# Reordering the first five steps of a fused attention and gated-convolution kernel: input transposes ahead of the attention output, output transposes one step later, weight preparation later

## Chip, cores and metric

One core of one Trainium2 chip. The metric is the device time of one execution in microseconds (us), the median of several executions. Engines: PE is TensorE (matrix products and transposes), PEld its weight loads, DVE is VectorE, ACT is ScalarE, POOL is GpSimd. DMA moves data between device memory and on-chip memory.

Runs carry a state. A run is called slow when it lies over 1.5% above the fastest run of the same kernel. Ratios below use fast runs alone, and compare with the kernel before in the same round; the rounds ran on different chips.

## The reference, cut to what matters

```python
def _attn_ref(q, k, v):                 # 8 batches, 8 heads, 576 positions, 64 wide
    scores = scale * np.matmul(q, k.transpose(0, 1, 3, 2))
    mask = block_i >= block_j           # causal in blocks of 64 positions
    scores = np.where(mask, scores, -1000000000.0)
    ...                                 # softmax over the last axis
    return np.matmul(attn, v)

def _moe_ref(x, w_val, conv_w, w_out):  # x: 8 x 576 x 512, from the heads side by side
    ...                                 # gate = sigmoid(causal convolution of 5 taps over positions)
    val = x @ w_val
    return (gate * val @ w_out)
```

The inputs and the result are float32.

## The kernel before

All instructions are issued in an order that the program fixes. One step `p` of 32 handles a pair of heads: three score tiles S0, S1 and S2 with their exponentials, the transposes of the next pair, and the attention output ("av") of the pair before. Half a batch of the convolution and the products with `w_val` and `w_out` follow from step 5 (`LAG`) on.

```python
def trans(p, bank): ...      # PE: 8 transposes of cast q and k; VectorE copies them into qkT
def s_tile(p, t): ...        # PE: score tile t; ScalarE: exponential into pt
def mask(p): ...             # GpSimd: two memsets on pt, after the third exponential of p
def av(p, banks): ...        # PE: 30 matmuls; VectorE: reciprocal and scaling, twice, into x16
def xtrans(p, bank): ...     # PE: 5 transposes of x16; VectorE copies them into xt
def trans_tails(b, bank):... # PE: 4 transposes of the last 64 positions of a batch; VectorE copies to kt
def s_last(b): ...           # last scores of a batch, and their exponential
def conv_weights(): ...      # PE turns the convolution weights, VectorE builds DG from them

def casts(p):                # all on GpSimd, in this order
    for i in (p + 1, p + 2):
        if ... and (p >= 5 or i == p + 1):
            cast_qk(i)       # q and k of a pair, 128x1024, float32 to float16
    cast_v(p)
    ...
    if p == 3 or (p > 0 and p % 4 == 0 and p + 4 < NP):
        cast_tails((p + 4) // 4, nc.gpsimd)
    if p in (6, 7):
        cast_w_out(p - 6)

for p in range(NP):          # NP = 32
    gs = p - LAG
    ...
    casts(p); s_tile(p, 0); s_tile(p, 1)
    ...                      # p == 0: warm-ups and tails instead of av
    av(p - 1, ...)
    trans(p + 1, 2)          # for 0 < p < 31
    ...                      # permute_w_out at 8, 9, 10; output tiles from 11 on
    s_tile(p, 2); mask(p)
    ...                      # p == 0: warm-ups, conv_weights, trans(1), last scores
    ...                      # even gs: convolution
    xtrans(p - 1, ...)
    if p in (5, 6):
        scale_w_val(2 * p - 10); scale_w_val(2 * p - 9)   # VectorE: w_val * 0.5 into w_val_sb
    ...                      # val, permute_w_out(1) at 8, tails, last scores at 4
```

`warm(n)` are n dummy matmuls that keep PE busy.

The softmax here doesn't subtract the row's maximum and nothing guards it: scores larger than these inputs give would overflow.

## Time and profile before

| | before |
|---|---|
| median of 3 runs | 198.56 us (198.2 to 198.68) |
| profiled run | 198.43 us, span 196.6 us, mean granted clock 0.996 |
| first score matmul of step 1, 5, 9, 31 | 14.26, 29.53, 52.10, 165.40 us |

How to read it: the span is cut into 40 equal slices of 4.9 us, one digit each, in tenths (9 means 90% or more). The row of the granted TensorE clock, from the page of the kernel before, is what the prediction did not show:

```profile
PEclk9999999999999999999999999999999999999998
```

The granted clock is 0.9 or more in every slice but the last, which has 0.8. The loop that the prediction finds in steps 2 to 4 shows on GpSimd. In the timeline of the kernel before the columns are start, duration, engine, line, operation, output and input, shape; the bracket is the idle time before and what ended it. L204 is the mask and L129 the cast of q and k.

```profile
21.70 0.41 POOL L204 MEMSET pt<- 64x384 f16 x1 [1.63 <-ACT pt L188]
22.32 1.04 POOL L129 CAST qk<-qks 128x1024 f16<-128x1024 f32 x1
...
25.62 0.41 POOL L204 MEMSET pt<- 64x384 f16 x1 [1.14 <-ACT pt L188]
```

From mask to mask 3.92 us pass.

### The profile page before, as it was taken

To read this page: it belongs to the slowest core of one execution; us is meant where nothing else is said; L and a number is where in the kernel's file an instruction comes from. 1 tells how busy PE (TensorE), PEld (TensorE's weight loads), DVE (VectorE), ACT (ScalarE), POOL (GpSimd) and SP (SyncE) were. 2 spreads that over 40 slices of the span, in tenths; PEclk is the share of its full clock that TensorE was granted. 3 is DMA by queue.
4 is the path that set the end of the run, shared out by engine and by line. 5 is a ranking of instruction groups with operands and counts; after the bars stand their busy time and mean duration, and the time that the engine had idled before them with its cause. 6 is when DMAs were issued, how large, how long until landed. Compare 5 with 4: busy or idle time off the path is not lost.

```text
span 196.6 us, 8730 instructions
## 1 busy us (share of the span) xinstructions
PE 183.3 (93%) x3714; PEld 124.4 (63%) x3714; DVE 130.8 (67%) x286; ACT 138.6 (71%) x192; POOL 83.5 (42%) x168
## 2 busy tenths in 40 slices
PE   2999878779899999999999999999999999999992
PEld 1456656557577676667766677677767676755550
DVE  4346785897678686777686877768676868642451
ACT  4438778758699778877888878887988787635321
POOL 7363664596444554345434644464445422100000
PEclk9999999999999999999999999999999999999998
DMA  5999999999899568876887687977775111124445
GB/s 155 256 286 265 250 274 323 312 215 278 242 224 253 171 174 217 255 228 186 236 232 234 189 240 212 276 216 207 220 213 146 57 56 58 58 107 165 163 160 213
DMA packets 70337, 40.43 MB, mean 206 GB/s; under 512 B 48149, under 2 KB 64789, under 8 KB 70298
## 3 DMA queue, kind: packets, MB, share of 16 engines
q1 hardware_dynamic: 69872, 39.46, 73.8%
q8 instruction: 29, 0.48, 1.0%
q10 hardware_dynamic: 426, 0.40, 0.6%
q14 instruction: 10, 0.08, 0.2%
HBM read 30.42 MB, written 9.44 MB: 203 GB/s over the span
## 4 chain that ended last, share of the span: by engine, by line
PE 80%; DVE 10%; POOL 3%; ACT 2%; DMA 2%; issue 1%; POOLq 0%; SPq 0%; DVEq 0%; ACTq 0%
PE G L33 51%; PE S L33 18%; PE G L154 6%; PE G L244 5%; DVE qkT L165 3%; DVE x L235 3%; DMA vs<-in_v_dram 2%; POOL qk L129 1%; ACT pt L188 1%; PE G L141 1%; DVE w_val L379 1%; DVE rc L234 1%; DVE gv L282 1%; POOL v L134 1%; POOL pt L204 1%
## 5 line engine op out<-in xcount | busy, mean ns | idle before, releaser
L188 ACT ACTIVATE pt<-S 128x1024 f16<-128x1024 f32 x96 | 95.0, 1024 | 21.4 <-PE S L33 19.1
L204 POOL MEMSET pt<- 64x384 f16 x32 | 13.5, 423 | 74.0 <-ACT pt L188 73.9
L33 PE MATMUL G<-xt,w_val 128*128 128x288 f16 x256 | 37.9, 286 | 0.3 <-DVE qkT L165 0.2
L165 DVE COPY qkT<-G 128x1024 f16<-128x1024 f16 x31 | 37.7, 1215 | 0.2 <-PE G L154 0.2
L129 POOL CAST qk<-qks 128x1024 f16<-128x1024 f32 x31 | 32.9, 1061 | 10.9 <-DMA qks<-in_k_dram 7.7
L33 PEld LDWEIGHTS <-pt 128*128 128x128 f16 x960 | 31.2, 97 | 8.6 <-issue 4.0
L33 PE MATMUL G<-w_out,gv 128*128 128x512 f16 x144 | 36.5, 379 | 0.0
L33 PE MATMUL G<-v,pt 128*128 128x65 f16 x896 | 34.1, 194 | 1.7 <-DVE gv L282 1.3
L282 DVE SCALAR_TENSOR_TENSOR gv<-th,G 128x288 f16<-128x288 f32 x64 | 28.2, 453 | 10.7 <-PE G L33 9.0
L304 ACT COPY osb<-G 128x512 f32<-128x512 f32 x31 | 18.2, 586 | 23.8 <-PE G L33 22.0
L235 DVE TENSOR_TENSOR x<-G,rc 128x320 f16<-128x320 f32 x64 | 31.5, 492 | 2.2
L33 PEld LDWEIGHTS <-qkT 64*128 64x128 f16 x496 | 16.0, 94 | 22.9 <-issue 16.8
L33 PE MATMUL S<-qkT 64*128 64x512 f16 (+1 forms) x248 | 28.5, 301 | 2.1 <-DVE qkT L165 1.1
L33 PEld LDWEIGHTS <-w_val 128*128 128x128 f16 x256 | 24.2, 98 | 8.5 <-issue 0.9
L234 DVE RECIPROCAL rc<-G 128x5 f32<-128x5 f32 x64 | 12.2, 190 | 22.6 <-PE G L33 22.5
L246 DVE COPY xt<-G 128x576 f16<-128x576 f16 x32 | 14.6, 455 | 13.5 <-PE G L244 13.2
L154 PE MATMUL G<-ident,qk 128*128 128x128 f16 x256 | 20.1, 222 | 0.2 <-POOL qk L129 0.2
L134 POOL CAST v<-vs 128x512 f16<-128x512 f32 x32 | 19.9, 621 | 0.5 <-DMA vs<-in_v_dram 0.3
L33 PEld LDWEIGHTS <-gv 128*128 128x128 f16 x144 | 12.9, 98 | 9.9
L33 PE MATMUL G<-xt,DG 32*32 32x288 f16 x640 | 17.2, 288 | 0.0
L33 PE MATMUL S<-xt,DG 32*32 32x288 f16 x640 | 17.1, 287 | 0.0
L154 PEld LDWEIGHTS <-qk 128*128 128x128 f16 x256 | 15.4, 100 | 1.3 <-POOL qk L129 0.4
(58 smaller groups left out, 151.8 us busy)
## 6 DMA issues: line engine op xcount, KB each, us to landing
out_dram<-osb SPq DMA_DIRECT2D x35, 256.0 KB, 2.1
qks<-in_q_dram SPq DMA_DIRECT2D x32, 256.0 KB, 4.2
vs<-in_v_dram SPq DMA_DIRECT2D x64, 128.0 KB, 4.4
qks<-in_k_dram SPq DMA_DIRECT2D x31, 256.0 KB, 4.3
tlst<-in_q_dram SPq DMA_DIRECT2D x8, 128.0 KB, 4.8
tlst<-in_k_dram SPq DMA_DIRECT2D x8, 128.0 KB, 4.6
vtst<-in_v_dram SPq DMA_DIRECT2D x8, 128.0 KB, 4.8
w_st<-in_moe_w_val_dram SPq DMA_DIRECT2D x2, 512.0 KB, 6.3
```

The costliest lines, as they stand in the source:

```text
L33: nc.tensor.matmul(out=out, lhsT=lhsT, rhs=rhs, start=start, stop=stop, skip_group_check=True)
L129: nc.gpsimd.tensor_copy(out=o, in_=s)
L134: nc.gpsimd.tensor_copy(out=v16s[p % NV][0:128, 0:4, 0:2, 0:64], in_=s)
L154: nc.tensor.transpose(out=r[:, o:o + 128], in_=t[0:128, c, 2 * i:2 * i + 2, 0:64], identity=ident16[0:128, 0:128])
L165: nc.vector.tensor_copy(out=o[0:128].rearrange("p i (s n) -> p i s n", n=4), in_=src)
L188: nc.scalar.activation(out=pts[p % NPT][0:128, 0:2, 512 * t:512 * t + 512], in_=s[0:128, 0:2, 0:512], func=AF.Exp, bias=0.0, scale=0.125)
L204: nc.gpsimd.memset(pt[64:128, 0:2, 0:1536].rearrange("p h (t s) -> p h t s", t=3)[:, :, :, 0:64], 0.0)
L234: nc.vector.reciprocal(out=rc[0:128], in_=O[:, :, 64:65])
L235: nc.vector.tensor_tensor(out=x[0:128, 0:5, h, 0:64], in0=O[:, :, 0:64], in1=rc[0:128].to_broadcast([128, 5, 64]), op=ALU.mult)
L246: nc.vector.tensor_copy(out=xts[b % NX][0:128, g, 4:4 + SEQ], in_=r[:, 0:SEQ])
L282: nc.vector.scalar_tensor_tensor(out=gv[u][0:128, x, bi, hf, 0:288], in0=t[0:128, x, 0:288], scalar=1.0, in1=r[0:128, 0:288], op0=ALU.add, ...
L304: nc.scalar.copy(out=o[0:128], in_=r[0:128, 0:512])
```

## The change

The intent: transposes of the next pair are issued ahead of av, so that VectorE copies them without first normalising av; output transposes are taken from the pair before last, so that PE doesn't wait for that normalisation. Convolution weights leave step 0, and the `w_out` work is moved later. The core of the diff, with cuts marked:

```diff
     def casts(p):
+        if p == 3 or (p > 0 and p % 4 == 0 and p + 4 < NP):
+            cast_tails((p + 4) // 4, nc.gpsimd)
         for i in (p + 1, p + 2):
 ...
-        if p == 3 or (p > 0 and p % 4 == 0 and p + 4 < NP):
-            cast_tails((p + 4) // 4, nc.gpsimd)
-        if p in (6, 7):
-            cast_w_out(p - 6)
 ...
+    for p in range(LAG):
+        loads(p)
+        casts(p)
+        s_tile(p, 0)
+        s_tile(p, 1)
+        if p == 0:
+            warm(2)
+            trans_tails(0, 0)
+        if p > 2:
+            trans_tails(p - 2, 0)
+        if p > 0:
+            trans(p + 1, 2)
+        if p > 1:
+            xtrans(p - 2, 3)
+        if p > 0:
+            av(p - 1, (0, 1))
+        s_tile(p, 2)
+        mask(p)
+        if p == 0:
+            trans(1, 2)
+            warm(2)
+        if p in (0, 3):
+            s_last(p // 3)
+        if p < 2:
+            warm(4 - 2 * p, 3)
+        if p == 2:
+            conv_weights()
 ...  # second loop, from step 5: as before, but
+        if 9 <= p <= 12:
+            permute_w_out(p - 9, 3)
+        if p > 12:
+            out(3)
 ...
+        if p in (7, 8):
+            cast_w_out(p - 7)       # after the mask
 ...
+        if p == 5:
+            scale_w_val(0)
+            scale_w_val(1)
 ...  # ahead of val in step 5; the other two after val in step 6
+        if p == 6:
+            scale_w_val(2)
+            scale_w_val(3)
```

## The prediction

> **What bounds the kernel now.** I read the page first: busy shares, then the forty slices.
>
> ```profile
> PE 183.3 (93%) x3714; PEld 124.4 (63%) x3714; DVE 130.8 (67%) x286; ACT 138.6 (71%) x192; POOL 83.5 (42%) x168
> ...
> PE   2999878779899999999999999999999999999992
> ...
> DMA  5999999999899568876887687977775111124445
> ```
>
> Over the whole span TensorE (PE) is the busiest engine, and from slice 13 on (about 59 us) its row is all nines. Before that it has 7s and 8s: these first nine or so steps ("step" p handles one pair of heads, 32 in all) are another regime, and the change touches only it. What the change is worth is therefore how much earlier or later the saturated stretch starts, plus or minus TensorE work moved across that border. DMA is also at nine tenths there, so input may arrive too late for a faster start.
>
> Next the busy time in stretches cut at the first score matmul of steps 1 to 9 (columns: PE, PEld, DVE, ACT, POOL, clock, DMA share, GB/s).
>
> ```profile
> 14.26:18.00 3.74, 3.51 (x63) 2.34 (x63) 2.47 (x6) 2.96 (x3) 0.15 (x1) 1.00 1.24 264
> 18.00:21.74 3.74, 2.97 (x59) 2.17 (x60) 2.77 (x7) 2.96 (x3) 2.04 (x5) 1.00 1.24 259
> 21.74:25.48 3.74, 3.24 (x63) 2.40 (x63) 2.77 (x7) 2.94 (x3) 2.67 (x5) 1.00 1.16 235
> 25.48:29.53 4.05, 3.49 (x72) 2.58 (x73) 3.35 (x9) 2.98 (x4) 3.33 (x6) 1.00 1.09 292
> ...
> 39.86:46.32 6.46, 5.05 (x149) 3.72 (x149) 5.47 (x11) 4.22 (x6) 5.07 (x9) 1.00 0.96 231
> ```
>
> No engine is full in steps 1 to 4, though each takes 3.74 to 4.05 us: a chain of waits sets the pace. PE idles 42.94 - 36.96 = 6.0 us between 14.26 and 57.20, the most that perfect ordering could win there. The chain of waits inside steps 2 to 4 names the loop:
>
> ```profile
> 22.32 1.05 POOL qk L129
> 23.37 0.05 issue
> 23.42 0.62 PE G L154 x8
> 24.04 0.35 PE S L33 x10
> ...
> 24.48 1.03 ACT pt L188
> ...
> 25.62 0.05 POOL pt L204
> ...
> 26.23 1.04 POOL qk L129
> ```
>
> GpSimd casts q and k of the next pair (L129), PE transposes them (L154), PE makes the third score tile S2, ScalarE takes its exponential, GpSimd masks it (L204, L206), and only then comes the next cast, because on GpSimd the mask of step p stands ahead of the cast of step p+1. From cast to cast: 26.23 - 22.32 = 3.91 us. (In steps 1 and 2 the VectorE loop of normalising and copying qkT costs nearly the same, 3.74.)
>
> [...] the transposes of step 3 start at 23.42 just after the cast ended at 23.37, and all later matmuls of the step come after them. [...] a transposition placed ahead of other matmuls makes these wait for its cast too. [...] the trace shows a cold start (four warm-up matmuls 1.89 us) and three later ones in 0.82; [...] so I expect no cold clock from fewer warm-ups. [...] one cast took 1.69 us instead of 1.04 while the convolution weights were built on VectorE (11.97 to 12.80).
>
> **The change, part by part.** The order of instructions in the built kernel confirms what the diff says: in steps 1 to 4 PE runs S0, S1, transposes of pair p+1, output transposes of pair p-2, attention output (av) of pair p-1, S2. GpSimd still has the mask of p-1 ahead of the cast of p+1.
>
> 1. Step 0. Convolution weights (about 1.0 us on PE) and 10 of 26 warm-up matmuls (0.22 to 0.27 us each, from 1.25 us for five and 0.82 for three) go. S0 of step 1 then starts when the filler has run: S2 of step 0 done 9.75, transposes 10.2, two warm-ups 10.65, last scores 10.9, four warm-ups 11.8. Before: 14.26. A head start of about **2.4 us**.
>
> 2. Steps 1 to 4. The good: qkT no longer waits for normalisation on VectorE (4 instructions, 0.20 + 0.49 + 0.18 + 0.49 us). The bad: in the loop above, between transposes and S2, there now stand five output transposes (0.3 us of issue) and av (30 matmuls, 1.0 us, 22.28 to 23.3). New loop: mask 0.65 with its wait, cast 1.05, wait 0.1, transposes 0.5, output transposes 0.3, av 1.0, S2 with its wait 0.5, exponential 1.02 = **5.1 us** against 3.9. In steps 3 and 4 the cast of the tails (0.62) is moved ahead of the cast, on the loop: 5.7. Ends of the third exponential, from 11.07 in step 0 (before: 11.26): step 1 15.9 (before 17.73), step 2 21.05 (21.58), step 3 26.7 (25.50), step 4 32.9 (29.41). The tails of step 4 land at about 28, which adds 0.4. The before side still spent 0.6 us on the last scores of batch 1 in step 4; I have these inside step 3. So after step 4 the changed kernel is some **2.7 us behind** at the first exponential of step 5 (32.9 against 30.23).
>
> 3. Steps 5 to 7. Most of that is given back, as the old kernel stalls here: GpSimd waits 2.37 us for qk of pair 7 (lands 33.5) and 2.08 for pair 8 (38.2), and step 7's av starts only at 41.77, after GpSimd had cast w_out (1.24) ahead of the mask and VectorE had scaled w_val (1.85) ahead of gv. The DMA stream is full and no load waits for a buffer, so landings stay. Behind by 2.7 us, the new kernel finds pair 7 nearly there. My walk: third exponential of step 5 ends 36.65 (before 33.70), of step 6 41.25 (39.0); mask of step 6 done 41.95, av at 42.3 against 41.77: **0.5 us behind**. Then the two moved w_val scalings (1.3 to 1.85) delay normalisation of step 7 and its convolution, which reuses the banks of av: **+0.9**.
>
> 4. Steps 8 to 12. Step 8 loses two w_out permutations (2 x 0.33) and the stall on their copy (0.69): 5.78 becomes about 4.4. First score matmul of step 9: 52.1 to 52.3, against 52.10. But the two permutations remain to be done in the saturated part: 0.66.
>
> 5. The end. Outputs start two steps later, so two more tiles (4 matmuls, 0.97 us each) sit in the tail. PE is full there too, so they only move: 0.
>
> Sum: 0.0 to 0.2 + 0.66 = about **+0.7 us**, 198.56 + 0.7 = 199.3.
>
> **Rivals.** (a) *The head start survives.* If transposes ran without waiting for the cast, steps 1 to 4 would go at the ScalarE pace (three exponentials, 3.0 us, plus gaps) and the 2.4 us of step 0 would be kept, perhaps with more of the 6.0 us of idle: 194 to 196.5. For it: qk of pairs 3 and 4 land at 14.2 and 16.9, long before use. Against: the fixed order on GpSimd. And pairs 7 and 8 land at 33.5 and 38.2 regardless; with casts blocking in order on GpSimd, nearly all of a lead would be waited away, so about 197. (b) *The delay persists.* If the deferred weights collide with steps 5 to 8 more than I see, 2.7 us of lag plus 0.9 stays: 201.5 to 202. For it: VectorE is at 5.47 of 6.46 us in step 7. Against: cast w_out no longer precedes the mask. (c) *Nothing moves:* DMA sets the start of saturation and both orders fit under it: 198.0 to 199.0. This is near to my own result.
>
> **Range and chances.** 2% is 4.0 us. Faster by that needs more than the whole step-0 gain and no DMA wait: 3%. Slower by it needs the entire lag to persist and grow: 5%. The range takes my walk's likely error of 2 us either way, a little more above since such a walk omits small waits: 197.0 to 202.0.
>
> **What would show it.** Step 1's S0 near 11.8; casts of q and k from step 2 on 5 us apart instead of 3.9, PE idle before the transposes of steps 2 to 4 released by the cast, 1 us or more each; third exponential of step 4 ending near 32.9; the GpSimd waits for pairs 7 and 8 shrinking from 2.4 and 2.1 to below 1; av of step 7 starting without a wait for gv; no wait on the copy of w_out near 51; all nines from about 52 us. Wrong would be: step intervals below 4 us in steps 2 to 4 (rival a), or step 9's scores after 54 us (rival b).

## The result

| | before | after |
|---|---|---|
| median of 4 runs each | 198.38 us | 204.10 us (203.28 to 205.35) |
| profiled run | 198.43 us, clock 0.996 | 205.35 us, clock 0.972 |
| first score matmul of step 1, 5, 9, 31 | 14.26, 29.53, 52.10, 165.40 | 12.08, 35.56, 57.52, 170.58 |

The ratio is 1.030, interval 1.024 to 1.037: slower. (A ratio is the mean time of one kernel's fast runs over that of the other's of the same rounds, so not quite the ratio of the medians.) All four runs of the changed kernel count as fast, with mean clocks of 0.972, 0.975, 0.958 and 0.983.

The page of the changed kernel: busy tenths of PE and the granted clock.

```profile
PE   3896677778999999999999999999999999999992
PEclk9997876999999999999999999999999999999999
```

The sevens of PE go further right than before, and the clock row has gained 7, 8, 7, 6 in slices 4 to 7. Next, stretches of the changed kernel, cut at the first score matmul of steps 1 to 4. The columns are stretch and length, then the busy time of PE, PEld, DVE, ACT and POOL with instruction counts, the clock, the DMA share and GB/s.

```profile
12.08:15.35 3.27, 2.95 (x59) 2.02 (x58) 1.65 (x3) 2.37 (x3) 1.49 (x2) 1.00 1.17 290
15.35:22.32 6.97, 5.33 (x68) 4.50 (x68) 3.59 (x9) 3.44 (x4) 2.16 (x4) 0.76 1.14 244
22.32:29.83 7.51, 4.79 (x72) 3.98 (x72) 4.27 (x9) 3.01 (x4) 3.09 (x5) 0.77 1.02 257
29.83:35.56 5.73, 4.57 (x63) 3.72 (x64) 2.71 (x6) 2.38 (x3) 3.27 (x6) 0.70 1.12 334
```

Where the kernel before took 3.74 to 4.05 us a step, steps 2 and 3 take 7.0 and 7.5. No engine is full in them, and the clock is at about three quarters on average. The chain of waits in step 3 (start, duration, what):

```profile
23.88 1.05 POOL qk L129
24.93 0.05 issue
24.98 0.99 PE G L154 x8
25.97 0.53 PE G L244 x5
26.50 1.65 PE G L33 x30
28.15 0.52 PE S L33 x10
...
28.75 1.03 ACT pt L188
```

This is the predicted loop with output transposes (L244) and av (30 matmuls, L33) between the transposes (L154) and S2. But the prediction had 0.5, 0.3 and 1.0 us for these three, and they took 0.99, 0.53 and 1.65. The granted clock in this trace has two values, 1.00 and 0.50, and changes between 18.24 and 35.30 us in pieces of 3.41 us. Cutting the changed kernel at their edges:

```profile
14.82:18.24 3.42, 1.78 (x21) 0.79 (x18) 1.25 (x5) 2.85 (x3) 2.12 (x4) 1.00 1.24 264
18.24:21.65 3.41, 3.41 (x51) 3.17 (x48) 2.83 (x6) 0.46 (x1) 0.04 (x1) 0.50 1.06 239
21.65:25.06 3.41, 1.76 (x19) 1.17 (x19) 1.43 (x3) 2.50 (x3) 2.66 (x5) 1.00 0.90 236
25.06:28.48 3.42, 3.42 (x53) 3.27 (x55) 2.41 (x6) 0.00 (x0) 0.42 (x1) 0.50 1.07 252
28.48:31.89 3.41, 1.47 (x27) 0.63 (x21) 0.70 (x2) 3.08 (x4) 1.93 (x4) 1.00 1.10 329
31.89:35.30 3.41, 3.13 (x43) 3.06 (x43) 2.18 (x5) 0.37 (x1) 1.34 (x3) 0.50 1.13 322
```

In these six windows the pattern alternates. In one PE waits for GpSimd and ScalarE and is busy for 43 to 52%. In the next it has the burst of transposes, output transposes, av and S2 to do, and does it at a clock of 0.50. The longest single PE idle in these steps is 1.39 us. In the kernel before the emptiest such window held 2.06 of 3.41 us (60%), and the clock was 1.00 in it and in the one after it:

```profile
38.22:41.63 3.41, 2.06 (x19) 1.11 (x19) 3.41 (x5) 2.55 (x4) 3.27 (x4) 1.00 0.95 257
```

How far each kernel is behind the kernel before (the start of a step's first score minus that of the kernel before; the last column is the difference of spans; one profiled run each). The profile of fill, in italics, is of a slow run: only its first two columns, ahead of its first half-clock window, are used.

| kernel | step 1 | step 5 | step 9 | step 31 | end |
|---|---|---|---|---|---|
| after | -2.2 | 6.0 | 5.4 | 5.2 | 6.9 |
| *fill* | -1.6 | 2.7 | 4.0 | 3.3 | 5.0 |
| av_first | -2.3 | 3.3 | 2.9 | 3.5 | 5.2 |
| before_swap | 0.6 | 4.1 | 4.0 | 3.9 | 3.9 |
| two_ahead | -1.6 | 3.7 | 3.2 | 4.2 | 6.0 |
| tails_last | -1.6 | 5.2 | 3.4 | 2.5 | 4.2 |
| undo_both | -2.3 | 0.8 | -1.6 | -2.0 | -0.2 |
| defer_only | 0.4 | 0.4 | -1.5 | -2.2 | -0.4 |
| delay | 0.0 | 2.8 | 0.3 | 0.2 | 0.2 |
| loop_fill | 0.1 | 3.5 | 3.3 | 4.6 | 4.7 |
| best1 | -2.3 | 0.2 | 1.0 | 1.4 | 3.1 |
| best2 | -1.8 | -1.6 | -2.6 | -2.4 | -0.7 |

### The profile page after: what moved, and what is told of

Same layout as the page of the kernel before. It is cut to its first block, busy times and chain, and to the rows that moved or that the text cites. A ratio compares the mean times of both kernels' runs of the same rounds, so it can differ in the third digit from the quotient of the medians.

```text
span 203.5 us, 8700 instructions
## 1 busy us (share of the span) xinstructions
PE 185.4 (91%) x3704; PEld 127.9 (63%) x3704; DVE 131.5 (65%) x286; ACT 138.4 (68%) x192; POOL 82.9 (41%) x168
## 4 chain that ended last, share of the span: by engine, by line
PE 77%; DVE 8%; DMA 5%; POOL 3%; ACT 3%; issue 2%; SPq 1%; POOLq 0%; DVEq 0%; ACTq 0%
PE G L33 47%; PE S L33 17%; PE G L154 6%; PE G L244 5%; DMA qks<-in_k_dram 5%; DVE qkT L165 3%; POOL qk L129 3%; DVE x L235 2%; ACT pt L188 2%; DVE gv L282 1%; DVE rc L234 1%; DVE w_val L377 1%; PE G L141 1%; POOL pt L206 0%; SPq L86 0%
## 5 line engine op out<-in xcount | busy, mean ns | idle before, releaser
L33 PE MATMUL G<-xt,w_val 128*128 128x288 f16 x256 | 38.2, 286 | 0.5 <-DVE qkT L165 0.4
L33 PEld LDWEIGHTS <-pt 128*128 128x128 f16 x960 | 33.7, 101 | 6.7 <-issue 4.5
L33 PE MATMUL G<-v,pt 128*128 128x65 f16 x896 | 36.3, 199 | 0.1
L33 PE MATMUL G<-w_out,gv 128*128 128x512 f16 x144 | 36.3, 379 | 0.0
L129 POOL CAST qk<-qks 128x1024 f16<-128x1024 f32 x31 | 32.3, 1043 | 4.9 <-DMA qks<-in_k_dram 3.4
L33 PE MATMUL S<-qkT 64*128 64x512 f16 (+1 forms) x248 | 29.0, 303 | 2.9 <-ACT pt L188 2.3
L33 PEld LDWEIGHTS <-qkT 64*128 64x128 f16 x496 | 16.1, 95 | 23.5 <-issue 18.9
L33 PEld LDWEIGHTS <-w_val 128*128 128x128 f16 x256 | 24.2, 98 | 8.9 <-issue 1.2
L154 PE MATMUL G<-ident,qk 128*128 128x128 f16 x256 | 20.9, 228 | 3.0 <-POOL qk L129 2.9
L33 PEld LDWEIGHTS <-gv 128*128 128x128 f16 x144 | 13.0, 98 | 10.1
L154 PEld LDWEIGHTS <-qk 128*128 128x128 f16 x256 | 15.9, 102 | 4.6 <-POOL qk L129 4.0
L33 PE MATMUL G<-xt,DG 32*32 32x288 f16 x640 | 17.2, 288 | 0.7 <-DVE x L235 0.3
L33 PE MATMUL S<-xt,DG 32*32 32x288 f16 x640 | 16.8, 287 | 0.1
```

The source lines that it names most:

```text
L33: nc.tensor.matmul(out=out, lhsT=lhsT, rhs=rhs, start=start, stop=stop, skip_group_check=True)
L129: nc.gpsimd.tensor_copy(out=o, in_=s)
L154: nc.tensor.transpose(out=r[:, o:o + 128], in_=t[0:128, c, 2 * i:2 * i + 2, 0:64], identity=ident16[0:128, 0:128])
```

## The experiments

Four questions: is the half clock a cause; which of the two reorderings (PE order, tails first) lengthens the loop; what happens to a lag in steps 5 to 8; and is there a version that beats both. Each edit is against the changed kernel unless it says otherwise.

### fill: dummy matmuls in the idle time of PE

```diff
         s_tile(p, 0)
+        if p == 4:
+            warm(4, 2)
         s_tile(p, 1)
 ...
+        if p > 1:
+            warm({2: 5, 3: 4, 4: 2}[p], 2)
         if p > 2:
             trans_tails(p - 2, 0)
+            warm(2, 2)
```

> The changed kernel with 15 dummy matmuls put where TensorE waits in steps 2 to 4 (5 ahead of the transposes of step 2; 4 and 2 around the tail transposes of step 3; 4 between the score tiles, 2 and 2 around the tail transposes of step 4). Nothing else moves. Theory A (the waits of the longer loop leave TensorE half idle for one clock window after another[...]): granted clock back to 0.99, no half-clock windows, third exponential of step 4 ending near 33 instead of 36.8, time 199 to 201 us. Theory B (the half clock is a side effect; the order alone costs the 5.7 us): 203 to 205 us, or slower still by the 15 dummies (about 3 us).

(The text on record says 15 dummies; the edit issues 19.) Measured: two of four runs kept a full clock (1.0) and took 199.88 and 201.66 us; the other two had one half-clock window or so (clock 0.988, 0.990), took 203.39 and 204.54 us and count as slow. The fast runs give a ratio of 1.012 (1.005 to 1.019), against 1.030 for the changed kernel. So more work on PE took 1.8% off, which is 3.6 us of 198.5: this is my estimate of what the half clock costs, from two fast runs. The profile fell on a slow run, whose first half-clock window (0.50) came only at 39.92; up to there it shows the order at full clock. The third exponential of step 4 ends at 33.5 us, as theory A expected, against 36.85 in the changed kernel, and step 5 starts at 32.19, 2.7 us behind the kernel before. That is the lag that the prediction had for this place. (That half-clock window isn't left over from the loop: the window before it, 46% busy, holds a gap in issue of 1.75 us, of the kind described under loop_fill.)

### av_first: the old order on PE, all else of the change kept

```diff
+        if p > 0:
+            av(p - 1, (0, 1))
         if p > 2:
             trans_tails(p - 2, 0)
 ...
-        if p > 0:
-            av(p - 1, (0, 1))
         s_tile(p, 2)
```

> The changed kernel with one thing undone: in steps 1 to 4 the attention output stands ahead of the input transposes again. Theory A (the transposes ahead of the attention output make TensorE wait for the cast, which waits for the mask, so the loop grows from 3.9 to over 5 us and the clock falls): casts about 4.2 to 4.8 us apart, clock above 0.99, time 196.5 to 199 us, at or below the kernel before. Rival C (it is the other parts: output transposes one step later, tails cast ahead, deferred weights, fewer warm-ups): still above 202 us.

Measured: 203.15 us, ratio 1.021 (1.015 to 1.028), with clocks of 0.975 to 0.991: theory A's time is missed and rival C's is met. Undoing the order on PE alone doesn't repair it. GpSimd's timeline in this run, at the cast of the tails (L115) in steps 3 and 4:

```profile
21.76 0.62 POOL L115 CAST tl<-tlst 128x512 f16<-128x512 f32 x1 [1.54 <-DMA tlst<-in_k_dram]
...
29.23 0.62 POOL L115 CAST tl<-tlst 128x512 f16<-128x512 f32 x1 [2.16 <-DMA tlst<-in_k_dram]
```

With the loop quicker again, the tails had not landed when GpSimd came to them, and being first in its queue they hold up the cast of q and k behind them. In the changed kernel this wait doesn't show, because its loop is already later than the landings. A slow loop hid the second fault.

### before_swap: only the order on PE, in the kernel before

```diff
+        elif gs < 0:
+            trans(p + 1, 2)
+            av(p - 1, (0, 1))
         else:
-            av(p - 1, (0, 1) if cv or gs < 0 else (1, 0))
-        if 0 < p < NP - 1:
+            av(p - 1, (0, 1) if cv else (1, 0))
+        if LAG <= p < NP - 1:
             trans(p + 1, 2)
```

> The kernel before with one thing done: in steps 1 to 4 the input transposes stand ahead of the attention output. Theory A: the loop grows by the 1.0 us of the attention output to about 4.9 us, TensorE waits over 1 us for the cast in each of steps 2 to 4, at least one half-clock window appears; 200 to 204 us. Rival C: within 1 us of the kernel before.

Measured: 202.15 us, ratio 1.019 (1.015 to 1.023), with a clock of 0.999 to 1.0 in three of four runs. GpSimd's masks in this run:

```profile
18.42 0.41 POOL L204 MEMSET pt<- 64x384 f16 x1 [3.60 <-ACT pt L188]
...
23.19 0.41 POOL L204 MEMSET pt<- 64x384 f16 x1 [2.54 <-ACT pt L188]
...
28.02 0.41 POOL L204 MEMSET pt<- 64x384 f16 x1 [2.05 <-ACT pt L188]
```

From mask to mask 4.77 and 4.83 us, against 3.9 before: the order alone puts av on the loop and costs nearly 1 us a step at full clock, without any fault of the clock or of the tails. Its lag of 4.1 us at step 5 is still 4.0 at step 9 and 3.9 at the end.

### two_ahead: cast q and k of two pairs ahead from step 1

```diff
-            if i < NP and i not in qkT and i not in qk16 and (p >= 5 or i == p + 1):
+            if i < NP and i not in qkT and i not in qk16 and (p >= 1 or i == p + 1):
```

> The changed kernel, with q and k cast two pairs ahead on GpSimd from step 1 on, not from step 5: the cast then no longer stands behind the mask of the step before, so the loop mask, cast, transposes, attention output, exponential is cut, at the price of waiting for the DMA earlier. Theory A: transposes of steps 2 and 3 start without a wait for a cast, third exponential of step 2 ends near 19.6 instead of 22.2, clock above 0.99, casts wait for pairs 5 and 6 instead; time 196.5 to 199.5 us. Rival C: above 202 us.

Measured: 203.25 us, ratio 1.022 (1.016 to 1.028). The transposes of steps 2 and 3 no longer wait for their cast, as meant. But the loop, taken off that path, ran into the tails. First the PE timeline of this run, then its windows at the edges of the clock:

```profile
29.48 0.40 PE L141 MATMUL G<-ident,tl 128*128 128x128 f16 x4 [3.17 <-POOL tl L115]
```

```profile
26.39:29.81 3.42, 0.33 (x6) 0.33 (x7) 0.00 (x0) 1.47 (x2) 0.67 (x2) 1.00 1.06 301
29.81:33.22 3.41, 3.41 (x57) 3.25 (x55) 2.86 (x7) 0.00 (x0) 2.10 (x3) 0.50 1.04 297
```

PE stands for 3.17 us at the transposes of the tails, and a window at 0.50 follows. Theory A's time is missed here too.

### tails_last: only the tails put back behind the other casts

```diff
     def casts(p):
-        if p == 3 or (p > 0 and p % 4 == 0 and p + 4 < NP):
-            cast_tails((p + 4) // 4, nc.gpsimd)
 ...                                  # and the same two lines after cast_vtail
-        if p > 2:
-            trans_tails(p - 2, 0)
 ...                                  # after mask(p):
-        if p in (0, 3):
-            s_last(p // 3)
+        if p > 2:
+            trans_tails(p - 2, 1)
+        if p in (0, 4):
+            s_last(p // 4)
```

> The changed kernel with the tails treated as in the kernel before: their cast is again the last one of steps 3 and 4 on GpSimd, their transposes stand at the end of the step and the last scores of batch 1 in step 4. The transposes stay ahead of the attention output. Theory A2 (two parts are each enough to lose the time: the transposes ahead of the attention output, which make the loop 4.9 us, and the tails' cast ahead of the cast of q and k, which puts 0.6 us and the landing of the tails at 21.5 and 29 us on the loop): still slow from the first part alone, 201 to 203.5 us, casts of q and k 4.9 to 5.5 us apart, at least one half-clock window. Rival (the tails alone are the cause): 198 to 199.5 us.

Measured: 203.25 us, ratio 1.022 (1.015 to 1.029), clocks 0.966 to 0.996. Putting the tails back takes 0.8% off at the most likely value, but the intervals of this ratio and of the changed kernel's overlap; the long loop stays, with windows at 0.50 from 22.91 and from 29.74 us.

### undo_both: tails back and the old order on PE

The edit of tails_last, and this one:

```diff
         if p > 0:
+            av(p - 1, (0, 1))
             trans(p + 1, 2)
         if p > 1:
             xtrans(p - 2, 3)
-        if p > 0:
-            av(p - 1, (0, 1))
```

> As tails_last, and the attention output ahead of the transposes again: of the change there remain the shorter step 0, output transposes one step later, and the deferred weights. Theory A2: both causes are gone, so casts about 4.2 us apart, no half-clock window, 197 to 199.5 us. If one of the remaining parts is a cause of its own (output transposes, deferred weights): above 200.5 us.

Measured: 200.44 us (12 runs, 4 of them slow), ratio 1.005 (1.001 to 1.009). Either reordering is enough to cost about 2%, and undoing both brings back all but 0.5%. A likely part of what is left, which no run tests alone, shows in the PE timeline and in the windows of this run:

```profile
19.77 1.05 PE L33 MATMUL G<-ident,conv_nat 5*128 5x5 f32 x8 [1.30 <-DVE xt L246]
```

```profile
17.77:21.18 3.41, 2.11 (x31) 1.63 (x28) 2.23 (x5) 1.29 (x2) 1.47 (x3) 1.00 1.00 227
21.18:24.59 3.41, 3.41 (x49) 3.06 (x47) 2.70 (x6) 1.94 (x2) 1.84 (x3) 0.50 1.01 237
```

The convolution weights, moved to step 2, write the bank that the output transposes have just filled, and wait for VectorE to copy it. A window 62% full comes before one at 0.50 here.

### defer_only: only the later w_out and w_val work, in the kernel before

```diff
-        if p in (6, 7):
-            cast_w_out(p - 6)
 ...
-        if p in (8, 9, 10):
-            permute_w_out({8: 0, 9: 2, 10: 3}[p], 3)
-        if p > 10:
+        if 9 <= p <= 12:
+            permute_w_out(p - 9, 3)
+        if p > 12:
             out(3)
 ...
+        if p in (7, 8):
+            cast_w_out(p - 7)        # after the mask
 ...                                  # scale_w_val as in the changed kernel, permute at step 8 gone
```

> The kernel before with only the weights' parts of the change from step 5 on: casts and permutations of w_out later, the second half of the w_val scalings after the gate product, outputs from step 13 on. My prediction counted 1.3 + 0.7 us of stalls taken away in steps 6 to 8, 0.9 us of new stall in step 7 and 0.66 us of work moved later: so 197.3 to 198.8 us. Rival (the deferral itself costs, by the convolution of step 7 waiting for VectorE): 199.5 us or more.

Measured: 198.21 us (12 runs), ratio 0.997 (0.993 to 1.001). The deferral gains 1.5 us by step 9 and 2.2 by step 31, and gives most of it back in the end: its tail is longer, as windows from the first score of step 31 to the end show for the kernel before and the changed kernel, one line each.

```profile
165.40:196.60 31.20, 27.52 (x447) 16.59 (x446) 13.19 (x31) 13.23 (x24) 1.65 (x5) 0.98 0.38 142
```

```profile
170.58:203.50 32.92, 29.25 (x455) 17.37 (x454) 13.30 (x31) 14.41 (x26) 1.65 (x5) 0.99 0.41 151
```

Eight more matmuls (two output tiles) cost 1.72 us there.

### delay and loop_fill: the same lag made in two ways, in the kernel before

```diff
             s_last(1)                # end of step 4: delay
+            for _ in range(12):
+                mm(GT[3][0:128, 0:512], wz[0:128, 0:128], wz[0:128])
```

```diff
+        elif p < LAG:                # ahead of S2 in steps 1 to 4: loop_fill
+            for _ in range(4):
+                mm(GT[3][0:128, 0:512], wz[0:128, 0:128], wz[0:128])
         s_tile(p, 2)
```

> The kernel before with nothing but 12 dummy matmuls at the end of step 4, a delay of 12 x 0.215 = 2.6 us at full clock just ahead of the steps in which GpSimd waits for pairs 7 and 8. The step of my prediction that is on trial: a lag of 2.7 us after step 4 is mostly given back in steps 5 to 8, since the old kernel stalls there for DMA. If that is right: first scores of step 9 under 53 us against 52.1, time at most 0.8 us above the kernel before. If the waits of GpSimd are off the path: the lag stays, first scores of step 9 at 54.4 to 54.8, time 2.2 to 2.8 us above the kernel before.

> The kernel before with 4 dummy matmuls (0.86 us at full clock) between the transposes and S2 in steps 1 to 4: the loop of mask, cast, transposes and exponential is lengthened as by the attention output in before_swap, but TensorE stays busy and the order stays. It asks why the 2.8 us of the run delay were given back and the 4 us of before_swap were not. If a lag from the loop, in which all engines are late and not TensorE alone, is given back too: lag of 3 to 3.6 us at step 5, under 1.5 us at step 9, time at most 1.2 us above the kernel before. If such a lag is kept: 2.5 to 3.6 us at step 9, time 2 to 3.6 us above the kernel before. The clock stays above 0.995 in both cases.

Measured: delay 199.16 us (20 runs), ratio 1.005 (1.002 to 1.007); loop_fill 202.19 us, ratio 1.013 (1.002 to 1.023), at full clock in three of four runs. The delay of 2.8 us at step 5 is down to 0.3 at step 9. The lag of 3.5 us made inside the loop is 3.3 at step 9 in the one run profiled (1.5 more arise in its step 23). By the times less is kept: the other two runs at full clock, 201.15 and 201.34 us, lie 1.5 to 1.7 us above the mean of the fast runs of the kernel before in that round, 199.6, and the intervals of the two ratios overlap. Step 5 in both, in windows: delay first, then loop_fill.

```profile
32.32:36.43 4.11, 3.92 (x140) 3.18 (x140) 2.41 (x5) 3.39 (x5) 2.06 (x4) 1.00 1.09 319
```

```profile
33.06:38.85 5.79, 4.40 (x139) 3.07 (x140) 2.44 (x6) 4.09 (x6) 3.81 (x8) 1.00 1.12 323
```

While PE runs dummies after step 4, the other engines finish their work; GpSimd then has 2.06 us to do in step 5, ScalarE 3.39. When the loop itself is late, all engines are: 3.81 and 4.09. Besides, PE loses 1.29 us in this run inside the convolution to a gap that no wait in the profile explains ("issue" means that PE waited for nothing that the profile shows):

```profile
38.24 0.29 PE L33 MATMUL G<-xt,DG 32*32 32x288 f16 x1 [1.29 <-issue]
```

No run was made for these gaps. The PE timelines of 13 of the 18 profiles have gaps in issue of over 0.35 us, 15 in all, from 0.38 us (before_swap_ns) to 2.25 us (best2_two5), and all 15 end between 37.2 and 70.1 us. Those of the kernel before, delay, undo_both, delay_ns and after_ns have none. What makes them isn't shown. In step 23 of loop_fill PE idles for 1.30 us up to 133.21, which the profile puts down to ScalarE's th. In step 5 or 6, PE stands idle in issue for 0.83 us in the changed kernel (43.74), 0.84 in before_swap (40.76) and 1.29 in loop_fill (38.24). If all of that was on the path, which is the most that it can have cost, their lags at step 9 would otherwise have been 4.6, 3.1 and 2.0 us: more given back than the table shows, but not most of it.

### before_ns, before_swap_ns, delay_ns, after_ns: without the w_val scalings

After twelve runs it was still open what paces steps 5 to 8. Between the kernels with a short and a long stretch there, one thing differed along with it: the time of the four w_val scalings on VectorE. Two of them take 0.75 us in delay, where GpSimd is idle beside them, and 2.02 us in the changed kernel, beside GpSimd's casts.

```diff
+    nc.gpsimd.memset(w_val_sb[0:128], 0.02)     # at the start; the result is wrong on purpose
 ...
     def scale_w_val(x):
-        nc.vector.tensor_scalar(...)
+        pass
```

> The kernel before with the four w_val scalings on VectorE taken away (w_val is set to a constant on GpSimd during its first wait, so the result is wrong on purpose). From the first score of step 5 to that of step 9 the kernel before takes 22.57 us, of which the scalings take 3.18. Theory A (steps 5 to 8 are paced by VectorE's chain in program order, and the scalings, stretched by GpSimd's casts beside them, lie on it; the waits for the loads of pairs 7 and 8 do not): about 19.4 us for the stretch, near TensorE's own 18.7 of work, and 195.4 to 196.2 us in all. Theory B (the landing of pairs 7 and 8 at 33.5 and 38.2 paces these steps): 22.0 to 22.6 us for the stretch and 198 to 198.6 us in all.

> The kernel before with transposes ahead of attention output in steps 1 to 4, and without the scalings (wrong result on purpose). With them the stretch from step 5 to step 9 took 22.40 us, 3.39 of them scalings, and its lag of 4.1 us was kept. Theory A: 19.0 us for the stretch, so the lag against the kernel before without scalings is still 3.8 us at step 9: a lag of the loop is kept because nothing on the path of these steps waits for loads. About 199 us. Theory B (without the scalings in the way the lag would be waited away at the loads): the lag against the kernel before without scalings falls below 2 us at step 9.

> The kernel before with 12 dummy matmuls at the end of step 4, and without the scalings (wrong result on purpose). With them the stretch took 20.04 us, only 1.53 of them scalings, because GpSimd was idle beside them; the lag of 2.8 us fell to 0.26. Theory A (the delay was given back because VectorE's scalings no longer met GpSimd's casts): without the scalings nothing is left to be given back in that way, 18.5 us for the stretch, and a lag of some 1.9 us against the kernel before without scalings at step 9; 197.3 us. Theory B (the delay was absorbed by the waits for the loads): the lag is again 0.3 us or less at step 9.

> The changed kernel without the scalings (wrong result on purpose). With them its stretch from step 5 to step 9 took 21.96 us, 3.51 of them scalings (2.02 and 1.49 us for two pairs that take 0.75 each when GpSimd is idle). Theory A: 18.4 to 18.7 us for the stretch and about 200.7 us in all, if the half-clock windows of steps 2 to 4 stay as they were. Theory B (the stretch is held by the gaps in issue or by other waits): above 20.5 us for the stretch, above 202.5 us in all.

Measured: 199.42, 202.68, 201.65 and 204.84 us; ratios 1.006, 1.021, 1.016 and 1.029. No kernel became faster, because the edit has a cost of its own that I had not seen: beside the memset on GpSimd (4.51 to 6.32 us in before_ns) a VectorE cast took 2.06 us, where it took 0.43 in the kernel before (VectorE timelines: the kernel before, then before_ns), and step 1 then starts 1.4 to 3.2 us later than in the same kernel with its scalings.

```profile
4.68 0.43 DVE L127 CAST qk<-qks 128x512 f16<-128x512 f32 x1 [1.25 <-DMA qks<-in_k_dram]
```

```profile
4.54 2.06 DVE L127 CAST qk<-qks 128x512 f16<-128x512 f32 x1 [1.12 <-DMA qks<-in_k_dram]
```

So the totals decide nothing, and the stretches have to be read:

| step 5 to step 9, us | with scalings (their time) | without | theory A | theory B |
|---|---|---|---|---|
| before | 22.57 (3.18) | slow run, not used | 19.4 | 22.0 to 22.6 |
| before_swap | 22.40 (3.39) | 21.42 | 19.0 | |
| delay | 20.04 (1.53) | 20.03 | 18.5 | |
| after | 21.96 (3.51) | *20.29* (slow run) | 18.4 to 18.7 | above 20.5 |

Neither theory has its numbers. There is a floor at about 20 us that theory A lacked: with or without scalings, delay takes 5.05 to 5.09 us in each of steps 6 and 7. Above that floor, theory A has the right sign where the scalings were slow (before_swap loses 1.0 us, of which 0.15 are smaller gaps in issue: one of 0.84 us with scalings, 0.38 and 0.31 without) and the right zero where they were quick (delay loses 0.01). For the changed kernel the one profile is of a slow run, so its 1.7 us are an indication only; its steps 6 and 7 fall from 6.08 and 5.74 to 5.08 and 5.09. The 0.83 us gap in issue of the changed kernel's step 6 isn't in that run either, so these 1.7 us hold both. The delay tells one thing by its times alone: with scalings it costs 0.5% (0.9 us) against the kernel before, without them 1.0% (1.016 against 1.006, about 1.9 us). That suggests that a part of what it gave back came from scalings that no longer met GpSimd's casts, not from waits for loads. It isn't shown: the start of delay_ns is 0.3 us later than that of before_ns at step 1, its PE idles for 0.68 us up to 63.01, and the intervals are 0.5% wide.

### best1, best2, best2_two5: looking for a version that beats both

best1 is undo_both with the output transposes after S2 and the mask, casts of two pairs ahead from step 7 only, and the tails of batch 2 moved to step 5. best2 also puts the convolution weights in step 1 in place of two warm-ups, casts two ahead from step 9, and moves the transposes of those tails. best2_two5 is best2 with casts of two pairs ahead from step 5, as in the kernel before.

```diff
         if p > 0:
-            trans(p + 1, 2)
-        if p > 1:
-            xtrans(p - 2, 3)
-        if p > 0:
             av(p - 1, (0, 1))
+            trans(p + 1, 2)
         s_tile(p, 2)
         mask(p)
+        if p > 1:
+            xtrans(p - 2, 3)
 ...
-        if p == 2:
+        if p == 1:                   # best2
             conv_weights()
 ...
-            if ... and (p >= 5 or i == p + 1):
+            if ... and (p >= 9 or i == p + 1):   # best1: 7, best2: 9, best2_two5: 5
```

> A version for beating both: undo_both with the output transposes after S2 (off the loop), the tails of batch 2 cast and transposed in step 5 and not in step 4, and q and k cast two ahead only from step 7 on, so that no mask waits behind a cast that waits for pair 7 or 8. Theory A2: the head start of step 0 (2.2 us) is kept to step 5 and there is no wait for DMA ahead of a mask: 194.5 to 197 us. If the DMA stream sets the start of the saturated part: 197.5 to 198.5 us.

> best1 with three repairs that its trace asks for: the convolution weights in step 1 and not in step 2, where they waited 1.2 us for the copy of the output transposes out of the shared bank and made a half-idle clock window; the tail transposes of batch 2 in a bank of their own ahead of the w_val scaling, where they made the attention output of step 6 wait 1.34 us; q and k two ahead only from step 9. Theory A2[...]: no half-clock window, first scores of step 9 at 46 to 49 us against 52.1, 194 to 197 us. If the DMA stream or the steps from 5 on set the time: 197.5 to 199 us.

> best2, but q and k two ahead from step 5 on, as in both original kernels. If the cast that waits for pair 7 (lands at about 33.5 us) ahead of the mask of step 5 is what a head start runs into, this loses what best2 wins: first scores of step 9 at 50 to 51 us, 197 to 199 us. If that wait costs nothing: the same as best2 within 0.5 us.

Measured: best1 201.38 us, ratio 1.012 (1.004 to 1.020). Its convolution weights wait 1.20 us as in undo_both, av of step 6 waits 1.34 us for the copy of the tails, and a window at 0.50 follows each (from 20.53 after one 65% busy, from 37.60 after one 53% busy). best2 197.85 us (20 runs), ratio 0.995 (0.993 to 0.997), at full clock in most runs: half a per cent faster than the kernel before, which is under the 2% of a verdict "faster". It starts step 9 at 49.5 us, and its time lies in the range of the second case of its text, 197.5 to 199 us, not in theory A2's: a lead of 2.6 us at step 9 is 0.7 at the end. best2_two5 202.13 us, ratio 1.011 (1.007 to 1.015), slower than either range on record; its GpSimd, in the timeline:

```profile
30.41 1.04 POOL L129 CAST qk<-qks 128x1024 f16<-128x1024 f32 x1 [2.39 <-DMA qks<-in_k_dram]
34.45 1.04 POOL L129 CAST qk<-qks 128x1024 f16<-128x1024 f32 x1 [3.00 <-DMA qks<-in_k_dram]
```

Here the casts wait for loads ahead of the mask, PE waits for GpSimd, and a window at 0.50 follows at 37.84, after one 35% busy. (That profile fell on a slow run, which has a second half-clock window at 68.56 (mean clock 0.983), after a gap in issue of 2.25 us; the fast runs carry the ratio.) A lead of some 2 us at step 5 was worth little here, where the casts ahead of the mask waited 2.39 and 3.00 us for loads that came no sooner.

## Why the prediction was wrong, point by point

The prediction said 199.3 us and 5% for slower by over 2%; the changed kernel took 204.1 and is 3.0% slower.

**What held.** The head start of step 0: S0 of step 1 at 12.08 (predicted 11.8). The first loop: the third exponential of step 1 ended at 15.95 (15.9). The long loop at full clock: in fill the third exponentials of steps 1 to 4 end at 16.3, 21.4, 27.4 and 33.5 us, where the walk had 15.9, 21.05, 26.7 and 32.9, and the lag at step 5 is the 2.7 us of the prediction; even the late tails of step 4 are there (0.45 us of wait, 0.4 predicted). The wait for the loads of pairs 7 and 8 and the stall on the copy of w_out are gone from the changed kernel. The sign of the collision of w_val and casts held too.

**Step "so I expect no cold clock from fewer warm-ups": the walk reckoned with a full clock throughout; that failed, and it is the largest term.** Three windows at 0.50 came in steps 2 to 4, after windows in which PE was 52, 52 and 43% busy and never idle for more than 1.4 us at a time. They took the lag at step 5 from the expected 2.7 to 6.0 us in the profiled run, so 3.3 us there; the fast runs of fill against those of the changed kernel say 3.6. The busy share alone doesn't tell when it happens: in undo_both a window 62% busy came before one at 0.50, and in the kernel before one of 60%, in before_swap one of 55% was followed by 1.00. I could have been warned by the kernel before: its emptiest window was 60% busy, and I was about to empty several below that.

**Step 3, "most of that is given back": failed.** Predicted was a fall of the lag from 2.7 to about 0.1 us at step 9. The changed kernel went from 6.0 to 5.4, before_swap from 4.1 to 4.0, loop_fill from 3.5 to 3.3. Only delay, in which the other engines had caught up and PE met no gap in issue of over 0.35 us, gave its lag back. The prediction took waits of GpSimd for loads for slack on the path; their disappearance bought little. The scalings of w_val beside GpSimd's casts took 3.51 us in the changed kernel against 1.81 in undo_both, where the prediction had 0.9 us for their effect; the runs without scalings give 1.0 us for before_swap and, from a slow run, 1.7 for the changed kernel. This step is about 2 us short. Up to 0.8 us of it is PE's gap in issue at 43.74 (0.83 us). That the scalings make a difference between the two kernels isn't shown: the kernel before spends 3.18 us on them.

**Steps 4 and 5 of the working, "+0.66" and "they only move: 0": mis-sized.** From step 9 to the end the changed kernel lost 6.9 - 5.4 = 1.5 us, so 0.8 us more than I had. Two output tiles in the tail cost 1.7 us, as expected. But steps 11 and 12, from which they were taken, shrank only from 5.61 and 4.91 to 5.60 and 4.61 us, where 0.64 us each was to be saved (an output tile of 0.97 against a permutation of 0.33). In step 11 there is a gap in issue (at 71.00, 0.60 us from one start to the next, 0.31 of it idle; tails_last, without it, takes 5.09 us); why step 12 gave only 0.30 is open.

**The tails.** The cast of the tails is on the loop, as predicted with 0.62 us: it took 0.99 us in step 3, beside VectorE's building of the convolution weights, and 0.61 in step 4. It met no late landing there. In kernels with a quicker loop it did: 1.54 and 2.16 us in av_first. As a danger the landing was underrated; in this kernel it was not what cost.

**The sum**, for the profiled runs: 0.7 predicted, 3.3 for the clock, about 2.0 for what was not given back, 0.8 for the end: 6.8 us, of 6.9 measured. **Rival (b)**, "the delay persists", with 201.5 to 202 us, was nearer. It lies where before_swap and loop_fill at full clock do; no rival had the clock.

**Open.** How the 2.0 us of steps 5 to 8 divide between slow scalings, gaps in issue and a lag that simply stays; the run that would show it for the changed kernel was a slow one. What makes the gaps in issue: no run tests it. The shares of the order and of the tails can't be cut apart exactly, as the half-clock windows fall differently in each run.

## What to carry to other kernels

Draw the cycle of waits across engines before reordering one of them: work that moves between a cast and the product which releases the next cast goes on the loop, even if its own wait disappears. Where a change leaves PE half idle in bursts, look at the granted clock window by window, in both kernels: here windows 43 to 52% busy had the next burst at 0.50, which cost about 3.6 us (my estimate from the fast runs of fill). Where PE stands still without a wait on record, set the size of the gap against the term to be explained, as with the 0.83 us at 43.74, and call its cause open until a run tests it. Idle time of a side engine at a load isn't slack for the whole loop until a run with a plain delay, and one with the loop itself slowed, have both shown it.
